# Ranking the experts of the second MoE on the chip: two short experts with weights fetched by computed address

## The chip, the cores and the metric

The kernel runs on one core of one Trainium2 chip. The metric is the device time of one execution in microseconds (us), as the median of several runs. A core has five engines that run side by side, each with a queue of its own that it works off in order: PE (TensorE, the matmuls; its weight loads are shown apart as PEld), DVE (VectorE), ACT (ScalarE), POOL (GpSimd) and SP (SyncE, which here only issues DMAs). Sixteen DMA engines move data for all queues.

## The reference: what is computed

Three stages follow each other, all in fp32. First comes an attention with 4 batches, 8 heads, 576 positions and head size 64, in which each query keeps its 32 largest scores. Its output, 2304 tokens of width 512, goes through a first "MoE" that has one expert for all tokens (512 to 2048 to 512). Then comes the second MoE, which the change is about:

```python
logits = x @ w_gate                       # 8 experts
expert_idx = np.argmax(logits, axis=1)    # one expert per token
...
for e in range(E):
    mask = expert_idx == e
    xe = x[mask]
    h = np.maximum(xe @ w1[e], 0.0)       # 512 -> 1024
    ye = h @ w2[e]                        # 1024 -> 512
    out[mask] = gate_w[mask, None] * ye
```

Evaluated on the inputs that it draws, the reference sends 328, 333, 249, 289, 285, 189, 284 and 347 tokens to experts 0 to 7.

## The kernel before, in words

**Precision.** A matmul of the MoE stages is made of three passes: each operand is split into a high part `h` and a low part `l` of type fp32r, and h·h, h·l and l·h are accumulated. ACT makes the high part and DVE the low part.

**First MoE (`l1` L829, `l2` L860).** Tokens are worked in blocks of 256, and the hidden width in 16 chunks of 128. One step is one chunk: 12 matmuls of 128x256 for layer 1 (4 chunks of the input width, 3 passes) and 6 matmuls of 128x512 for layer 2 (2 token tiles, 3 passes). Between the two, ACT takes layer 1 out of PSUM (`gf`, `epi_a` L835), DVE and POOL finish it. The weights of layer 2 are read back from DRAM in each step (`wo`, L815, 512 KB). After each block `gate` works out the expert of each token, its place in that expert's list and its gate weight; the token's row goes to DRAM (`yd`, L917, 516 floats a row) and its number to a table in DRAM (`td`, L938). Each expert has a list of 2304 places there.

**Second MoE (L1128 to L1229).** Each expert gets `SLOTS` = 3 slots of 128 tokens (`CAP` = 384). The first 128 x 3 entries of each list form a table of 24 columns, `tab`, one column for each slot. The entries of the earlier blocks are read from `td` (`load_table`, L951: two reads and their minimum on DVE, L955); those of the last block are added in PSUM: `placed` holds, for each of its two token tiles, a matrix that says the place in a slot and one that says the slot, and PE multiplies them (L1133, L1135). DVE turns the sum into integers (`tabg`, `tab`, L1136, L1137). Then for each expert, in the order 0 to 7:

- `xgather(e)` (L1141): POOL fetches three tiles of 128 token rows by an indirect DMA (L1148).
- `xprep(e, j)` (L1152): four PE transposes per slot (L1157), ACT and DVE make the high and low part (L1159, L1160).
- `m2l1(e, f)` (L1165) for 8 chunks f of the hidden width: 12 matmuls of 128x384 into `lp`, which has two buffers (L1175); then ACT (L1179) and DVE (L1180).
- `m2l2(e, f)` (L1187): for each of 3 slots 3 matmuls of 128x512 (L1192). It runs two chunks behind `m2l1`.
- `m2out(e)` (L1194): ACT scales the three outputs (L1198), POOL scatters them to `out` (L1199).

**Weights of the second MoE.** An expert's two matrices come in 8 pieces of 512 KB, even numbers from `w1` and odd ones from `w2`. `wpiece(e, i)` (L963) takes one of 3 `raw` buffers, issues the load on SP (L967, L970), and has ACT and DVE split it (L977, L978). Six pieces of expert 0 are asked for in the last steps of the first MoE (L1116 to L1122). Pieces 5 and 7 are asked for after it, since their split parts lie in memory that the first MoE holds until it ends. After that, step (e, f) of the second MoE asks for piece f of expert e + 1 (L1228).

**Order.** The program gives each instruction a priority and a scheduler lays each engine's queue out ahead of time, so an instruction can stand in its queue well ahead of where the source has it, if the scheduler expects its data by then. On the chip each queue is then worked off in that order.

**End.** `control` (L1234) adds up the number of tokens beyond the slots and two other flags; a register load (L1300) decides whether a slow path runs. There, `more(cs, e, n)` (L1249) computes what is left of expert e, 128 tokens at a time, with weights that it loads by itself.

Of the kernel before, what the change touches and what calls it, by code (L numbers as in the profile page):

```python
# [57 lines left out]
def attention_two_moe_kernel(  # L58
# [36 lines left out]
    SLOTS = 3  # L95
    CAP = SLOTS * P
    NCK = 8
    CK = S // NCK

# [54 lines left out]
    def constants():  # L154
# [30 lines left out]
        G.iota(first, pattern=[[NT, NE], [P, SLOTS]], base=0, channel_multiplier=0, allow_small_or_imprecise_dtypes=True)  # L185
        c["tokm"] = tokm = cpool.tile([P, NTT], F32, name="tokm")
        G.iota(tokm, pattern=[[P, NTT]], base=-NT, channel_multiplier=1, allow_small_or_imprecise_dtypes=True)
        c["wg"] = wg = cpool.tile([P, NCC, NE], F32, name="wg")
# [9 lines left out]
    def body(cs, exact):  # L198
# [672 lines left out]
        def gate(bk, tt, y):  # L871
# [52 lines left out]
            if last:  # L924

                ad2 = m1p.tile([P, 1], I32, tag="ad2", bufs=2, name=f"ad2{i}")
                place, in128 = [wp[0].tile([P, n], F32, tag=f"oh{n}", bufs=2, name=f"oh{n}_{i}") for n in (P, NSL)]
                V.tensor_scalar(ad2, ad, P - 1, None, op0=ALU.bitwise_and)
                V.tensor_copy(sc[:, 4:5], ad2)
                V.tensor_tensor(sc[:, 5:6], sc[:, 3:4], sc[:, 4:5], op=ALU.subtract)  # L930
                V.tensor_scalar(place, cs["row"], sc[:, 4:5], None, op0=ALU.is_equal)
                V.tensor_tensor(sc[:, 6:7], cs["tokm"][:, i:i + 1], sc[:, 3:4], op=ALU.subtract)
# [14 lines left out]

        NSL = NE * SLOTS
        placed, gdone, trows, tables = [], [0], [], []

        def load_table():  # L951
            trows.extend(wp[0].tile([NSL, P], F32, name=f"trow{i}") for i in range(2))
            for a_, t_ in zip(trows, td):
                SP.dma_start(a_, t_.rearrange("(e s p) o -> e s (p o)", e=NE, p=P)[:, 0:SLOTS, :])
            V.tensor_tensor(trows[0], trows[0], trows[1], op=ALU.min)  # L955

# [4 lines left out]
        wst = {}  # L961

        def wpiece(e, i):  # L963
            kind, pc = i % 2, i // 2
            raw = wp[0].tile([P, 4 * FW], F32, tag="raw", bufs=3, name=f"raw{e}_{i}")
            if kind == 0:
                SP.dma_start(raw.rearrange("p (c f) -> p c f", c=NCC),  # L967
                             w1[e, :, pc * FW:(pc + 1) * FW].rearrange("(c p) f -> p c f", p=P))
            else:
                SP.dma_start(raw.rearrange("p (j n) -> p j n", j=FPP),  # L970
                             w2[e, pc * FW:(pc + 1) * FW, :].rearrange("(j p) n -> p j n", p=P))
            late = kind and pc >= NPC // 2
# [137 lines left out]
        wp[0] = m2.enter_context(tc.tile_pool(name="wp" + X, bufs=1, side="right"))  # L1110
        pre = []
        while gpos[0] < NG + 3 or pend:
# [16 lines left out]
        tab = tabp[0].tile([P, NSL], I32, name="tab")  # L1129
        tabg = tabp[0].tile([P, NSL], I32, name="tabg")  # L1130
        tps = ps2.tile([P, NSL], F32, tag="tp", bufs=2, name="tps")
# [33 lines left out]
        def m2l1(e, f):  # L1165
# [4 lines left out]
            fs = slice((f % FPP) * P, (f % FPP + 1) * P)  # L1170
            lp = ps2.tile([P, CAP], F32, tag="lp", bufs=2, name=f"lp{e}_{f}")
# [5 lines left out]
            hh = tabp[0].tile([P, CAP], F32R, tag="hh", bufs=3, name=f"hh{e}_{f}")  # L1177
            hl = tabp[0].tile([P, CAP], F32R, tag="hl", bufs=3, name=f"hl{e}_{f}")
            A.activation(hh, lp, AF.Relu)  # L1179
# [5 lines left out]
        def m2l2(e, f):  # L1185
            hh, hl = hst.pop((e, f))
            h, l = wst[e, 1, f // FPP]  # L1187
            ns = slice((f % FPP) * DM, (f % FPP + 1) * DM)
            for j in range(SLOTS):
                js = slice(j * P, (j + 1) * P)  # L1190
# [3 lines left out]
        def m2out(e):  # L1194
            gw = xst[e][2]
            for j in range(SLOTS):
                o = tabp[0].tile([P, DM], F32, tag="osb", bufs=3, name=f"osb{e}_{j}")
# [15 lines left out]
        for s in range(len(seq) + 2):  # L1213
            if s < len(seq):
                e, f = seq[s]
                if e + 1 < NE:
                    if f == (e == 0):
                        xgather(e + 1)
                    if 4 <= f < 4 + SLOTS:
                        xprep(e + 1, f - 4)  # L1220
# [13 lines left out]
    def control(cs, X):  # L1234
        with ExitStack() as st:
            ps = st.enter_context(tc.tile_pool(name="ctlp" + X, bufs=1, space=PSUM)).tile([1, 2 + NE], F32, name="ctlp")
            ctl, f = cs["ctl"], cs["ctlf"]
            PE.matmul(ps[:, 0:2], cs["one"], cs["flag"], start=True, stop=True)
            PE.matmul(ps[:, 2:2 + NE], cs["ones"][:, 0:1], cs["ohsum"], start=True, stop=True)
            cnt, over = f[:, 2:2 + NE], f[:, 2 + NE:2 + 2 * NE]  # L1240
            V.scalar_tensor_tensor(cnt, cs["iota8"][0:1, :], -float(NT), ps[:, 2:2 + NE], op0=ALU.mult, op1=ALU.add)
            V.tensor_scalar(over, cnt, float(CAP), 0.0, op0=ALU.is_gt, op1=ALU.add, accum_out=f[:, 0:1])
            V.tensor_scalar(over[:, 0:2], ps[:, 0:2], 1.0, 0.0, op0=ALU.mult, op1=ALU.add, accum_out=f[:, 1:2])
# [5 lines left out]
    def more(cs, e, n):  # L1249
        ident = cs["ident"]  # L1250
        with ExitStack() as st:
# [3 lines left out]
            for nm, src, m in (("1", w1, DM // P), ("2", w2, F2 // P)):  # L1255
# [5 lines left out]
                ws.append((h, l))  # L1261
            with tc.For_i(CAP, n, P) as i:
                row = [wp.tile([P, 1], F32, name=f"row{t_}") for t_ in range(len(td))]
# [37 lines left out]
    with tc.If(todo > 0):  # L1301
# [4 lines left out]
        for e in range(NE):  # L1306
            n = nc.values_load(ctl[0:1, 2 + e:3 + e], min_val=0, max_val=NT)
            with tc.If(n > CAP):
                more(cs, e, n)
# [30 lines left out]
```

## Time and profile before

| | |
|---|---|
| median of 3 runs | 1249.9 us (1246.48 to 1253.28) |
| profiled execution, own time | 1248.94 us |
| its span, first to last instruction | 1247.0 us |
| granted TensorE clock, mean | 0.961 of 2.4 GHz |
| PE busy | 1148.2 us (92%) |
| DVE, ACT, POOL busy | 940.1, 816.1, 461.8 us |
| HBM traffic | 180 MB, 144 GB/s over the span |

The profile has a page with totals and can be asked for parts of the span. In the rows below, "start us, us" are the start from the beginning of the span and the duration; "[3.14 <-ACT wh L977]" says that the engine was idle for 3.14 us before the instruction and what it was released by. An x12 is a count. The attention ends at about 871 us, the first MoE at 932, and the second MoE's matmuls run from 956 to 1232.

### The profile page before, as it was taken

To read this page: it belongs to the slowest core of one execution; us is meant where nothing else is said; L and a number is where in the kernel's file an instruction comes from. 1 tells how busy PE (TensorE), PEld (TensorE's weight loads), DVE (VectorE), ACT (ScalarE), POOL (GpSimd) and SP (SyncE) were. 2 spreads that over 40 slices of the span, in tenths; PEclk is the share of its full clock that TensorE was granted. 3 is DMA by queue.
4 is the path that set the end of the run, shared out by engine and by line. 5 is a ranking of instruction groups with operands and counts; after the bars stand their busy time and mean duration, and the time that the engine had idled before them with its cause. 6 is when DMAs were issued, how large, how long until landed. Compare 5 with 4: busy or idle time off the path is not lost.

```text
span 1247.0 us, 23972 instructions
## 1 busy us (share of the span) xinstructions
PE 1148.2 (92%) x7453; PEld 1033.9 (83%) x7453; DVE 940.1 (75%) x3800; ACT 816.1 (65%) x2089; POOL 461.8 (37%) x670
## 2 busy tenths in 40 slices
PE   6676788999999999999999999999986999999995
PEld 4565677788999899999888899998875999999994
DVE  4999999999999999999897999995423444444420
ACT  4888778687888887787777887784422444444421
POOL 5886555743323534323433323223433112221100
PEclk9678799999999999999999999999996999999998
DMA  3654556555544655645435545444954455555300
GB/s 81 201 163 137 181 187 207 156 140 144 148 125 126 141 155 161 141 124 135 129 99 153 145 121 155 121 121 125 315 170 136 147 171 172 154 163 164 121 19 26
DMA packets 184665, 180.22 MB, mean 145 GB/s; under 512 B 123933, under 2 KB 148813, under 8 KB 184528
## 3 DMA queue, kind: packets, MB, share of 16 engines
q1 hardware_dynamic: 178960, 167.24, 46.4%
q0 software_dynamic: 4416, 11.08, 2.9%
q8 instruction: 61, 1.00, 0.3%
q14 instruction: 76, 0.62, 0.2%
q10 hardware_dynamic: 1152, 0.28, 0.1%
HBM read 160.52 MB, written 19.59 MB: 144 GB/s over the span
## 4 chain that ended last, share of the span: by engine, by line
PE 74%; DVE 14%; ACT 5%; DMA 3%; issue 2%; POOL 2%; SPq 0%; POOLq 0%; ACTq 0%; DVEq 0%
PE l1ps L829 13%; PE yps L860 13%; PE lp L1175 11%; PE ops L1192 11%; PE ptps L755 9%; PE sps L596 5%; PE ptps L721 4%; DVE cd L626 2%; DVE pbuf L705 2%; DVE z L662 2%; DVE z L697 1%; PE ptps L888 1%; DMA raw<-in_moe_w_dram 1%; PE misc L440 1%; PE tp L1157 1%
## 5 line engine op out<-in xcount | busy, mean ns | idle before, releaser
L860 PE MATMUL yps<-wo,gh 128*128 128x512 f32 x576 | 216.3, 416 | 0.1
L264 POOL TENSOR_SCALAR gh<-gf 128x256 fp32r<-128x256 f32 x144 | 74.9, 520 | 348.9 <-PE yps L860 224.4
L626 DVE MAX8 cd<-sbuf 128x8 f32<-128x72 f32 x1152 | 187.9, 218 | 3.0 <-ACT sbuf L266 2.7
L829 PE MATMUL l1ps<-xh,wih 128*128 128x256 f32 x576 | 167.7, 291 | 8.7 <-DVE gf L841 6.6
L829 PE MATMUL l1ps<-xh,wil 128*128 128x256 f32 x576 | 163.8, 284 | 0.0
L829 PE MATMUL l1ps<-xl,wih 128*128 128x256 f32 x576 | 163.6, 284 | 0.0
L978 DVE TENSOR_TENSOR wl<-raw,wh 128x1024 fp32r<-128x1024 f32 x64 | 79.4, 1245 | 93.6 <-ACT wh L977 91.7
L755 PE MATMUL ptps<-vn,pt 128*128 128x65 f32 (+1 forms) x1152 | 145.1, 280 | 0.0
L755 PEld LDWEIGHTS ptps<-vn,pt 128*128 128x128 f32 x1152 | 142.4, 200 | 0.0
L705 DVE SCALAR_TENSOR_TENSOR pbuf<-sbuf,tall,pbuf 128x576 f32<-128x576 f32 x144 | 137.2, 953 | 0.2
L849 POOL TENSOR_TENSOR gl<-gf,gh 128x256 fp32r<-128x256 f32 x144 | 124.8, 867 | 11.3
L829 PEld LDWEIGHTS l1ps<-xh,wih 128*128 128x128 f32 x576 | 110.0, 191 | 20.1 <-DVE gf L841 12.3
L977 ACT ACTIVATE wh<-raw 128x1024 fp32r<-128x1024 f32 x64 | 67.7, 1059 | 83.4 <-PE lp L1175 40.2
L860 PEld LDWEIGHTS yps<-wo,gh 128*128 128x128 f32 x576 | 107.2, 189 | 16.0 <-POOL qh L452 0.3
L860 PE MATMUL yps<-wo,gl 128*128 128x512 f32 x288 | 116.6, 405 | 0.6 <-POOL gl L849 0.6
L687 ACT ACTIVATE jk<-sbuf,uall 128x576 bf16<-128x576 f32 x144 | 111.6, 775 | 4.1 <-DVE j L701 0.9
L678 ACT ACTIVATE pbuf<-sbuf,nb 128x576 f32<-128x576 f32 x144 | 111.1, 775 | 4.1 <-PE ptps L723 0.9
L829 PEld LDWEIGHTS l1ps<-xl,wih 128*128 128x128 f32 x576 | 110.1, 191 | 4.1
L266 ACT ACTIVATE sbuf<-sps 128x576 f32<-128x576 f32 x144 | 93.0, 646 | 29.9 <-PE sps L596 17.9
L721 PE MATMUL ptps<-ident,pbuf 128*128 128x128 f32 x576 | 93.7, 285 | 18.1 <-DVE j L701 10.2
L829 PEld LDWEIGHTS l1ps<-xh,wil 128*128 128x128 f32 x576 | 110.3, 192 | 0.1
L596 PE MATMUL sps<-kx,qh 128*128 128x288 f32 (+2 forms) x336 | 95.8, 318 | 15.0 <-ACT sbuf L266 11.1
(206 smaller groups left out, 3043.0 us busy)
## 6 DMA issues: line engine op xcount, KB each, us to landing
wo<-wod SPq DMA_DIRECT2D x144, 512.0 KB
raw<-in_moe_w_dram SPq DMA_DIRECT2D x64, 512.0 KB
vn<-in_v_dram SPq DMA_DIRECT2D x96, 128.0 KB
rawi<-in_moe_w_in_dram SPq DMA_DIRECT2D x16, 512.0 KB
rawo<-in_moe_w_out_dram SPq DMA_DIRECT2D x16, 512.0 KB
wod<-wc SPq DMA_DIRECT2D x16, 512.0 KB
qn<-in_q_dram SPq DMA_DIRECT2D x126, 64.0 KB
yd<-y SPq DMA_DIRECT2D x18, 258.0 KB
```

Source lines behind the costliest of these rows:

```text
L596: PE.matmul(d_, a_, b_, start=(i == 0), stop=(i == len(mm) - 1))
L626: V.max(cd[:, c, :], s[:, c * CK:(c + 1) * CK])
L678: A.activation(d["p"], d["s"], AF.Exp, bias=d["nb"], scale=SCALE)
L687: A.activation(jk, d["s"][:, 0:S], AF.Sign, bias=ts[t]["u"], scale=-1.0, accum_out=d["sg"])
L705: V.scalar_tensor_tensor(d["p"], d["s"], tall[:, t:t + 1], d["p"], op0=ALU.is_ge, op1=ALU.mult)
L721: PE.transpose(ptps[:, c * P:(c + 1) * P], pb[:, c0 + c * P:c0 + (c + 1) * P], ident)
L755: PE.matmul(d_, a_, b_, start=(i == 0), stop=(i == len(mm) - 1))
L829: PE.matmul(dst, a[:, c, fs], b_[:, c, :], start=(n == 0), stop=(n == 3 * NCC - 1))
L849: G.tensor_tensor(gl, gf, r_(gh), op=ALU.subtract)
L860: PE.matmul(yps[tt], a[:, tsl], b_, start=(f == 0 and m == 0), stop=(f == NF1 - 1 and m == 2))
L1175: PE.matmul(lp, a[:, c, fs], b_[:, c, :], start=(n == 0), stop=(n == 3 * NCC - 1))
L1192: PE.matmul(ops_[j], a[:, js], b_[:, ns], start=(f == 0 and m == 0), stop=(f == NF2 - 1 and m == 2))
```

## The change

The experts are worked in order of rank: expert 0 always comes first, then the others from the largest token count to the smallest (ties by number). The last two ranks have 2 slots of 128, not 3. Which expert has which rank is computed on the chip, so from rank 1 on the weight loads take the expert's number from a register of SP.

In `constants`, `tokm` goes and five small tables come (two iotas on POOL, eight small DVE operations). `load_table` drops the minimum on DVE; PE adds both table reads instead. After the first MoE:

```diff
+        rk = ps2.tile([P, 256], F32, name="rk")
+        cnt = rk[0:NSL, 0:NE]
+        PE.matmul(cnt, ones[:, 0:NSL], ohsum, start=True, stop=True)
+        key = place_[:, 0:NE]
+        V.tensor_tensor(key, cnt, cs["bias"], op=ALU.add)
+        V.scalar_tensor_tensor(place_[:, NE:2 * NE], key, 1.0, own, op0=ALU.mult, op1=ALU.mult, accum_out=rank[:, 1:2])
+        V.tensor_scalar(place_[:, 2 * NE:3 * NE], key, rank[:, 1:2], 0.0, op0=ALU.is_gt, op1=ALU.add, accum_out=rank[:, 0:1])
+        V.tensor_scalar(rank[:, 2:3], rank[:, 0:1], float(SLOTS), part[:, 0:1], op0=ALU.mult, op1=ALU.add)
+        V.tensor_scalar(place_, cs["row"][0:NSL, 0:NSL], rank[:, 2:3], None, op0=ALU.is_equal)
+        tq = ps2.tile([NSL, P], F32, tag="tp", bufs=2, name="tq")
+        for i, a_ in enumerate(trows):
+            PE.matmul(tq, ident[0:NSL, 0:NSL], a_, start=(i == 0), stop=False)
+        for i, (a_, b_) in enumerate(placed):
+            PE.matmul(tq, b_, a_, start=False, stop=(i == len(placed) - 1))
+        V.scalar_tensor_tensor(trows[0], tq, part[:, 3:4], cs["row"][0:NSL, :], op0=ALU.subtract, op1=ALU.subtract)
         tps = ps2.tile([P, NSL], F32, tag="tp", bufs=2, name="tps")
-        PE.matmul(tps, trows[0], ident[0:NSL, 0:NSL], start=True, stop=False)
-        for i, (a_, b_) in enumerate(placed):
-            PE.matmul(tps, a_, b_, start=False, stop=(i == len(placed) - 1))
+        PE.matmul(tps, trows[0], place_, start=True, stop=True)
         V.tensor_scalar(tabg, tps, float(NT - 1), None, op0=ALU.min)
         V.tensor_copy(tab, tps)
+        PE.matmul(rk[0:1, 16:16 + NE], part[:, 1:2], place_.rearrange("p (e s) -> p e s", s=SLOTS)[:, :, 0], start=True, stop=True)
+        V.tensor_copy(cs["list"], rk[0:1, 16:16 + NE])
+        for r in range(1, NE):
+            turn[r] = nc.values_load(cs["list"][0:1, r:r + 1], engines=[mybir.EngineType.SP], min_val=0, max_val=NE - 1)
```

The load of a piece is parted from its split, and takes its address from `turn`:

```diff
+        def wload_(e, i, after=None):
+            kind, pc = i % 2, i // 2
+            at_ = slice(e, e + 1) if e == 0 else ds(turn[e], 1)
+            wraw[e, i] = raw = wp[0].tile([P, 4 * FW], F32, tag="raw", bufs=3, name=f"raw{e}_{i}")
+            if after is not None:
+                G.tensor_copy(raw[:, 0:1], after[:, 0:1])
+            if kind == 0:
+                SP.dma_start(raw.rearrange("p (c f) -> p c f", c=NCC),
+                             w1[at_, :, pc * FW:(pc + 1) * FW].rearrange("o (c p) f -> p (o c) f", p=P))
...
         def wpiece(e, i):
             kind, pc = i % 2, i // 2
...
+            if (e, i) not in wraw:
+                wload_(e, i)
+            raw = wraw.pop((e, i))
...
-            if gpos[0] > NG - 12 and len(pre) < NPC + NPC // 2:
-
-                pre.append(2 * len(pre) if len(pre) < NPC else 2 * (len(pre) - NPC) + 1)
-                wpiece(0, pre[-1])
+            if gpos[0] > NG - 13 and len(pre) < NPC + NPC // 2:
+
+                if len(wraw) == 3 or len(pre) + len(wraw) == NPC + NPC // 2:
+                    pre.append(order[len(pre)])
+                    wpiece(0, pre[-1])
+                if len(pre) + len(wraw) < NPC + NPC // 2:
+                    wload_(0, order[len(pre) + len(wraw)])
...
         xgather(0)
         for f_ in tables:
             f_()
+        for i in range(2 * NPC):
+            if i not in pre and (0, i) not in wraw:
+                wload_(0, i, xst[0][3][0])
         for i in range(2 * NPC):
             if i not in pre:
                 wpiece(0, i)
```

So pieces 5 and 7 of expert 0 are loaded only once the first gathered tile of expert 0 has arrived (`after`). In `xgather`, `xprep`, `m2l1`, `m2l2` and `m2out` the loops over slots and the widths follow the rank:

```diff
+    SHORT = 2
+    def slots(r):
+        return SLOTS - (r >= NE - SHORT)
...
+            w = slots(e) * P
+            lp = ps2.tile([P, CAP], F32, tag="lp", bufs=2, name=f"lp{e}_{f}")[:, 0:w]
...
-                    PE.matmul(lp, a[:, c, fs], b_[:, c, :], start=(n == 0), stop=(n == 3 * NCC - 1))
+                    PE.matmul(lp, a[:, c, fs], b_[:, c, 0:w], start=(n == 0), stop=(n == 3 * NCC - 1))
...
-            for j in range(SLOTS):
+            for j in range(slots(e)):
```

`control` counts a token as left over if it is beyond 384 in a long expert or beyond 256 in a short one; that takes one more small matmul on PE and three more DVE operations. `more` starts at place 256 for any expert that overflows.

## Rows read from the trace of the kernel before

**Rows 1.** The page: engines' totals, and the split of a weight piece on DVE.

```profile
PE 1148.2 (92%) x7453; PEld 1033.9 (83%) x7453; DVE 940.1 (75%) x3800; ACT 816.1 (65%) x2089; POOL 461.8 (37%) x670
...
L978 DVE TENSOR_TENSOR wl<-raw,wh 128x1024 fp32r<-128x1024 f32 x64 | 79.4, 1245 | 93.6 <-ACT wh L977 91.7
```

**Rows 2.** Windows: length, busy PE, PEld, DVE, ACT, POOL, PE clock, DMA share, GB/s.

```profile
940.00:950.00 10.00, 1.83 (x8) 1.53 (x7) 4.92 (x25) 2.00 (x2) 6.19 (x7) 0.50 0.52 90
...
1000.00:1100.00 100.00, 100.00 (x521) 90.57 (x520) 47.12 (x56) 44.87 (x65) 18.94 (x22) 1.00 0.51 157
```

**Rows 3.** Chain that ended last, 1000 to 1035 us: start, us, what.

```profile
1007.72 0.44 PE tp L1157 x4
...
1016.92 2.12 PE lp L1175 x12
...
1021.12 2.08 PE lp L1175 x12
...
1025.26 2.12 PE lp L1175 x12
```

**Rows 4.** Chain that ended last, 898 to 926 us.

```profile
922.24 1.39 PE yps L860 x6
923.62 1.42 PE l1ps L829 x12
```

**Rows 5.** Timeline of ACT, end of the first MoE.

```profile
904.34 0.48 ACT L835 ACTIVATE gf<-l1ps,three 128x256 f32<-128x256 f32 x1 [2.33 <-PE ptps L913]
...
910.28 1.06 ACT L977 ACTIVATE wh<-raw 128x1024 fp32r<-128x1024 f32 x1 [2.50 <-DMA raw<-in_moe_w_dram]
...
925.13 0.48 ACT L835 ACTIVATE gf<-l1ps,three 128x256 f32<-128x256 f32 x1 [2.33 <-PE l1ps L829]
...
943.77 2.00 ACT L977 ACTIVATE wh<-raw 128x1024 fp32r<-128x1024 f32 x2 [3.85 <-DMA td<-tok,ad]
...
966.02 1.06 ACT L977 ACTIVATE wh<-raw 128x1024 fp32r<-128x1024 f32 x1 [2.93 <-DMA raw<-in_moe_w_dram]
```

**Rows 6.** Timeline of DVE: table of slots, and an operation on 24x128.

```profile
922.46 0.28 DVE L955 TENSOR_TENSOR trow<-trow,trow 24x128 f32<-24x128 f32 x1 [1.97 <-DMA trow<-td]
...
941.66 0.69 DVE L933 TENSOR_SCALAR oh<-first,lsc 128x24 f32<-128x24 f32 x2
943.49 0.18 DVE L1136 TENSOR_SCALAR tabg<-tps 128x24 int32<-128x24 f32 x1 [1.14 <-DMA yd<-y]
```

**Rows 7.** Timeline of PE from the table to the second MoE.

```profile
940.75 0.59 PE L1133 MATMUL tps<-ident,trow 24*128 24x24 f32 x2 [0.45 <-DVE ad L923]
942.01 1.05 PE L1135 MATMUL tps<-oh,oh 128*128 128x24 f32 x4 [0.67 <-DVE oh L933]
950.86 1.09 PE L1157 MATMUL tp<-ident,xg 128*128 128x128 f32 x4 [7.80 <-POOL gw L1161]
952.67 2.25 PE L1157 MATMUL tp<-ident,xg 128*128 128x128 f32 x8 [0.72 <-DMA xg<-yd,tabg]
...
955.94 0.72 PE L1175 MATMUL lp<-xeh,wh 128*128 128x384 f32 x2
```

**Rows 8.** The register load at the end (L1300) on SP's queue: ns min/median/max.

```profile
L1300 SPq TENSOR_LOAD <-ctl x1: 554/554/554, 1234.2 to 1234.2; - x1
```

**Rows 9.** Timelines of POOL and SP: first gather, a weight load.

```profile
944.49 0.99 POOL L1148 DMA_INDIRECT xg<-yd,tabg  x1 [0.85 <-issue]
...
962.69 0.37 SPq L970 DMA_DIRECT2D raw<-in_moe_w_dram  x1
```

**Rows 10.** DMA queues in 950 to 956 us (packets, MB, share of 16 engines).

```profile
q0 software_dynamic: 305, 1.03, 49.8%
q1 hardware_dynamic: 750, 0.95, 43.9%
```

**Rows 11.** Timelines of DVE and POOL at the end.

```profile
1234.04 0.16 DVE L1245 CAST ctl<-ctlf 1x10 int32<-1x10 f32 x1
...
1234.40 0.97 POOL L1199 DMA_INDIRECT out_dram<-osb,tab  x1 [0.31 <-DVE ctl L1245]
```

More of the change, by code (lines that the diff above doesn't have):

```diff
@@ L96, in attention_two_moe_kernel @@
     CAP = SLOTS * P
+    SHORT = 2
+    NSL = NE * SLOTS
+    def slots(r):
+        return SLOTS - (r >= NE - SHORT)
     NCK = 8
@@ L185, in constants @@
         G.iota(first, pattern=[[NT, NE], [P, SLOTS]], base=0, channel_multiplier=0, allow_small_or_imprecise_dtypes=True)
-        c["tokm"] = tokm = cpool.tile([P, NTT], F32, name="tokm")
-        G.iota(tokm, pattern=[[P, NTT]], base=-NT, channel_multiplier=1, allow_small_or_imprecise_dtypes=True)
+        c["own"] = own = cpool.tile([NSL, NE], F32, name="own")
+        c["part"] = part = cpool.tile([NSL, 8], F32, name="part")
+        c["lead"] = lead = cpool.tile([NSL, NE], F32, name="lead")
+        c["bias"] = bias = cpool.tile([NSL, NE], F32, name="bias")
+        c["place"] = place = cpool.tile([NSL, NSL], F32, name="place")
+        G.iota(lead, pattern=[[-SLOTS, NE]], base=0, channel_multiplier=1, allow_small_or_imprecise_dtypes=True)
+        V.tensor_scalar(own, lead, float(SLOTS - 1), None, op0=ALU.is_le)
+        V.scalar_tensor_tensor(own, lead, 0.0, own, op0=ALU.is_ge, op1=ALU.mult)
+        V.scalar_tensor_tensor(place[:, 0:NE], lead, 1.0, own, op0=ALU.mult, op1=ALU.mult, accum_out=part[:, 0:1])
+        V.scalar_tensor_tensor(place[:, 0:NE], iota8[0:NSL, :], 1.0, own, op0=ALU.mult, op1=ALU.mult, accum_out=part[:, 1:2])
+        V.tensor_scalar(lead, lead, 0.0, None, op0=ALU.is_equal)
+        G.iota(part[:, 2:3], pattern=[[0, 1]], base=NT, channel_multiplier=NT // SLOTS, allow_small_or_imprecise_dtypes=True)
+        V.scalar_tensor_tensor(part[:, 3:4], part[:, 0:1], -float(NT - SLOTS * P) / SLOTS, part[:, 2:3], op0=ALU.mult, op1=ALU.add)
+        V.tensor_scalar(bias, iota8[0:NSL, :], -(NT + 1.0 / 16), None, op0=ALU.mult)
+        V.memset(bias[:, 0:1], 2.0 * NT)
+        c["list"] = cpool.tile([1, NE], I32, name="list")
         c["wg"] = wg = cpool.tile([P, NCC, NE], F32, name="wg")
@@ L961, in body @@
         wst = {}
+        wraw, turn = {}, {}
+        def wload_(e, i, after=None):
[7 more added lines that the diff above has]
+                             w1[at_, :, pc * FW:(pc + 1) * FW].rearrange("o (c p) f -> p (o c) f", p=P))
+            else:
+                SP.dma_start(raw.rearrange("p (j n) -> p j n", j=FPP),
+                             w2[at_, pc * FW:(pc + 1) * FW, :].rearrange("o (j p) n -> p (o j) n", p=P))
         def wpiece(e, i):
             kind, pc = i % 2, i // 2
[L965 to L971, printed above, removed]
+            if (e, i) not in wraw:
+                wload_(e, i)
+            raw = wraw.pop((e, i))
             late = kind and pc >= NPC // 2
@@ L1110, in body @@
         wp[0] = m2.enter_context(tc.tile_pool(name="wp" + X, bufs=1, side="right"))
-        pre = []
+        pre, order = [], [0, 2, 4, 6, 1, 3, 5, 7]
         while gpos[0] < NG + 3 or pend:
@@ L1188, in m2l2 @@
             ns = slice((f % FPP) * DM, (f % FPP + 1) * DM)
-            for j in range(SLOTS):
+            for j in range(slots(e)):
                 js = slice(j * P, (j + 1) * P)
@@ L1195, in m2out @@
             gw = xst[e][2]
-            for j in range(SLOTS):
+            for j in range(slots(e)):
                 o = tabp[0].tile([P, DM], F32, tag="osb", bufs=3, name=f"osb{e}_{j}")
@@ L1218, in body @@
                         xgather(e + 1)
-                    if 4 <= f < 4 + SLOTS:
+                    if 4 <= f < 4 + slots(e + 1):
                         xprep(e + 1, f - 4)
@@ L1235, in control @@
         with ExitStack() as st:
[L1236 removed]
+            ps = st.enter_context(tc.tile_pool(name="ctlp" + X, bufs=1, space=PSUM)).tile([1, 2 + 2 * NE], F32, name="ctlp")
             ctl, f = cs["ctl"], cs["ctlf"]
@@ L1239, in control @@
             PE.matmul(ps[:, 2:2 + NE], cs["ones"][:, 0:1], cs["ohsum"], start=True, stop=True)
+            V.tensor_scalar(cs["part"][:, 7:8], cs["part"][:, 4:5], NE - SHORT - 0.5, float(P), op0=ALU.is_gt, op1=ALU.mult)
+            PE.matmul(ps[:, 2 + NE:2 + 2 * NE], cs["part"][:, 7:8], cs["lead"], start=True, stop=True)
             cnt, over = f[:, 2:2 + NE], f[:, 2 + NE:2 + 2 * NE]
             V.scalar_tensor_tensor(cnt, cs["iota8"][0:1, :], -float(NT), ps[:, 2:2 + NE], op0=ALU.mult, op1=ALU.add)
-            V.tensor_scalar(over, cnt, float(CAP), 0.0, op0=ALU.is_gt, op1=ALU.add, accum_out=f[:, 0:1])
+            V.scalar_tensor_tensor(over, ps[:, 2 + NE:2 + 2 * NE], 1.0, cnt, op0=ALU.mult, op1=ALU.add)
+            V.tensor_scalar(over, over, float(CAP), 0.0, op0=ALU.is_gt, op1=ALU.add, accum_out=f[:, 0:1])
+            V.tensor_tensor(cnt, cnt, over, op=ALU.mult)
             V.tensor_scalar(over[:, 0:2], ps[:, 0:2], 1.0, 0.0, op0=ALU.mult, op1=ALU.add, accum_out=f[:, 1:2])
@@ L1261, in more @@
                 ws.append((h, l))
-            with tc.For_i(CAP, n, P) as i:
+            with tc.For_i((SLOTS - 1) * P, n, P) as i:
                 row = [wp.tile([P, 1], F32, name=f"row{t_}") for t_ in range(len(td))]
@@ L1307, in attention_two_moe_kernel @@
             n = nc.values_load(ctl[0:1, 2 + e:3 + e], min_val=0, max_val=NT)
-            with tc.If(n > CAP):
+            with tc.If(n > 0):
                 more(cs, e, n)
```

11 lines of the change are left out of this document (5 added, 6 removed).

## The prediction

> **What bounds the kernel now.** I read the page first, then the stretch of the second MoE by windows, then the chain of waits in it, and last the timelines of the two places where PE stands still.
>
> The page says that PE is busy 92% of the span, ahead of DVE with 75% [rows 1]. By windows, the second MoE is pure PE work: in 1000 to 1100 us PE is busy 100.00 of 100 us at full clock, DVE 47 and ACT 45 [rows 2]. The chain there alternates between layer 1 (12 matmuls, 2.08 to 2.12 us) and layer 2 (9 matmuls, the rest of a step); a step takes 4.17 us (4.20 from 1016.92 to 1021.12, then 4.14), and each gathered slot adds four transposes, 0.44 us [rows 3]. Whatever leaves PE's queue here leaves the time.
>
> PE stands still in two places. Near 910 us ACT waits for a weight piece to land (2.50 us) while the next `gf` stands behind it in ACT's queue, and PE waits for that `gf` [rows 5]. These are expert 1's first pieces, which the scheduler has drawn forward into the first MoE. Between 932 and 956 us the gate, the table and the first gathers run one after the other; in 940 to 950 us PE has 1.83 us of work and the clock is granted at 0.50, which is the 1.2 GHz level [rows 2].
>
> **The change part by part.**
>
> *Short experts.* 2 experts x 8 chunks = 16 steps. Each now has 12 matmuls of 256 columns and 6 of 512. That is exactly the mix of a step of the first MoE, and the trace has it: 1.42 + 1.39 = 2.81 us [rows 4]. So 4.17 - 2.81 = 1.36 us a step, 21.8 us in all, and 2 slots fewer to transpose, 0.9 us [rows 3]. PE is the bound here, so all of it counts: **-22.7**.
>
> The row says that 256 columns cost 0.118 us a matmul (1.42/12), 384 cost 0.174 (2.09/12 [rows 3]) and 512 cost 0.232 (1.39/6): proportional, no floor. The Trainium skill ("TensorE: Matmul & The Clock Gate", Back-to-back issue gap) gives another rule: the spacing of a stream is set by weight load and matmul together, about 81 ns at 128 columns and 131 ns at 512. By that slope, an estimate, 128 columns less would save only 17 ns a matmul, and layer 1 would give 3.2 us in place of 10.7. The trace disagrees at all three widths, so this gets the small chance below.
>
> *Pieces of expert 1.* Their address now comes from a register that is set only after the gate, so none can be drawn forward to 903 to 920 us. From the `gf` at 904.34 to the one at 925.13 are 6 steps, 20.79 us; undisturbed they would take 6 x 2.81 = 16.9 [rows 4, 5]. The stall of 3.9 us goes: **-3.9** (0 to -3.9). What is late next is nothing: with the loads gone only `wo` is fetched there. Loading expert 0's pieces earlier I cost at nothing: the scheduler already had them in the three `raw` buffers as soon as the attention's memory was free.
>
> *Table and ranking.* The table now takes one more round: DVE evicts 24x128 (0.28 by the operation of that shape), PE multiplies once more (0.59 for a matmul of 24 rows at the low clock), and PE hands to DVE (the matmuls of 942.01 end at 943.06, DVE starts at 943.49, so 0.43) [rows 6, 7]. That is 1.3. The two `placed` matmuls stream 128 columns, not 24; at the low clock four 128-column transposes take 1.09, so up to 0.5; I take 0.3. The ranking is one small matmul and five DVE operations of some 0.18, about 1.0; DVE idles 1.14 before `tabg` [rows 6], which covers most of it; if not, 1.0. I take 0.4. Sum **+2.0** (1.0 to 2.9). Everything behind `tabg` waits for this, the gathers first of all.
>
> *Register loads.* Seven on SP, each 0.55 [rows 8]: 3.9 us, and with some register arithmetic 4 to 5, after one more matmul and copy. Queued behind them on SP are pieces 5 and 7 of expert 0 and all later pieces; the gathers go through POOL and do not wait. SP is free again near 952 us.
>
> *Gathers.* From the issue of the first (944.49) to its transposes (950.86) pass 6.4 us [rows 7, 9], while in 950 to 956 us weight loads move 0.95 MB beside the gathers' 1.03 [rows 10]. Now pieces 5 and 7 wait for the first gather (by a copy on POOL, behind which stand only the gathers of the next expert) and the others for the registers. At the 0.33 MB/us that both moved, 0.95 MB is worth 2.9 us at the most. PE then is held by its own transposes and their evictions: of the stretch from 950.86 to 955.94 only 0.72 is spent waiting for a gather outright [rows 7]. I take half a microsecond more for the first gather itself: **-1.2** (0 to -2.9).
>
> *Late pieces.* Pieces 5 and 7 were split at 943.77 in the idle time [rows 5]. Now they are loaded near 952, land some 3.3 us later (issue 962.69, ACT 966.02 [rows 5, 9]), and the split, 1.06 on ACT [rows 5] and 1.2 on DVE [rows 1], lies beside PE-bound work. They are needed in step 6, about 25 us after the start; the two `lp` buffers give ACT about 2 us of slack. If they stand ahead of the first evictions in ACT's queue, PE waits for them: 0 to +8; I take **+0.7**, nearer to nothing, since a load of unknown landing is usually covered in rows such as the 2.93 at 966.02, where PE stayed busy.
>
> *Pieces for the last expert* have to come at one per 2.8 us, not 4.17. One turn of a buffer is 3.3 + 1.06 + 1.2 = 5.6 us, three buffers, so 1.9 us a piece. Enough, but ACT's waits of up to 2.93 us eat most of the slack: **+0.5** (0 to +11).
>
> *Start and end.* Eight small DVE operations at the start lie in DVE's wait for the first loads: 0 (to +1.3, eight of 0.16). At the end one scatter fewer takes 1.0 off POOL, but beside a slot of PE's that is 0.7 shorter and counted above, so 0.3 to 0.6 is left; `control` gets chained DVE operations of 0.16 and a matmul more, +0.5 [rows 11]. 0 (-0.6 to +0.6).
>
> **Sum:** -22.7 - 3.9 + 2.0 - 1.2 + 0.7 + 0.5 = -24.6. The profiled execution took 1248.9 (span 1247.0 and 1.9 around it), 1.0 below the median of 1249.9; from the one the sum gives 1224.3, from the other 1225.3. I say **1225**.
>
> **The rivals.**
>
> *The hand-over becomes the loss.* SP's register loads and the late pieces push the first steps back, pieces 5 and 7 stand before the first evictions on ACT: +10 over my terms, 1235. For it: ACT's queue is laid out ahead, and at 910 us it did wait in this way. Against it: the scheduler knows that these pieces come after the gather. 12%.
>
> *The seventh expert starves.* With 2.8 us steps the pieces of the eighth come late, ACT waits, and the step stays at 4.17: half of the 21.8 is lost, 1236. For it: ACT waits for `raw` today. Against it: 1.9 us a piece by the buffers, and the first MoE fetches 512 KB of `wo` in each 2.81 us step. 8%.
>
> *Weight loads set a floor under short matmuls.* 7.5 us less gain, 1232. The measured 1.42 for 12 speaks against it; 2%.
>
> *The slow path runs: slower.* The point is the 257th token in an expert of rank 7 or 8. Then `more` comes after the end: 4.2 MB of weights at 0.33 MB/us 12.7 us, splitting them 8 x 1.2 = 10, gather 6.4, transposes and evictions 2.4, 96 matmuls at 0.118 or less and 24 at 0.232 some 17, scatter 3: about 51 us, so 1276. For it: the mean is 288 tokens, and 249 is 7 away from 256. Against it: on its own inputs the reference's smallest counts are 249 and 189, and the trace of before has no instruction of `more`, so no expert was above 384. 3%.
>
> *More than I count* (the whole 2.9 of the gathers, a shorter end): below 1219, 3%.
>
> **How the numbers follow.** The forecast case has 72%, with 1219 to 1231 as its own range. To leave out no more than 2 in 10 the range goes from 1218 to 1236, so that it takes in the two cases at 1235 and 1236. A difference of 0.5%, 6 us, is about what can be told from no change here. Faster by more than that (below 1243.7): all cases but the slow path and the two losses together, 0.94; within it 0.03; slower 0.03.
>
> **What would show it.** Right: matmuls of 128x256 at L1175's successor, 64 per pass, 1.4 us per 12; short experts of some 23.5 us against 34.7; no weight piece on ACT from 900 us to the end of the first MoE, and `gf` every 2.81 there; `tabg` some 2 us after its old distance from the last DVE operation of the gate; seven register loads on SP, under 6 us. Wrong: PE idle inside the second MoE, longest where ACT waits for `raw`; a first `lp` over 16.6 us behind the last DVE operation of the gate (now 942.35 to 955.94, 13.6 [rows 6, 7]); any instruction of the slow path.

## The result, and the profile after

| | before | after |
|---|---|---|
| median (range) | 1250.7 us (1246.48 to 1253.28, 6 runs) | 1222.7 us (1216.34 to 1229.23, 6 runs) |
| span of the profiled execution | 1247.0 us | 1221.1 us |
| PE busy | 1148.2 us | 1127.4 us |

The changed kernel takes 0.9778 of the time before (95% interval 0.9756 to 0.9800). Predicted were 1225.0 us, with a range of 1218 to 1236: the measured 1222.7 us lies inside.

The two spans differ by 25.9 us. I cut both at events that both have: two `gf` of the first MoE on ACT, the first `lp` on PE, and the end of PE's last `ops`.

| stretch | before | after | difference |
|---|---|---|---|
| start to a `gf` of the first MoE | 872.79 | 874.29 | +1.50 |
| that `gf` to the last one | 55.16 | 51.54 | -3.62 |
| last `gf` to the first `lp` | 27.99 | 27.30 | -0.69 |
| first `lp` to the end of PE's work | 276.21 | 253.20 | -23.01 |
| rest | 14.85 | 14.77 | -0.08 |

The first row holds the attention, which the change leaves alone; in experiment 7 below, whose first two stages are the same, the last `gf` comes 2.7 us earlier than here, and I explain nothing with that row.

**The gates.** ACT's timeline at the end of the first MoE, where one `gf` came 20.79 us after another six steps earlier [rows 5]:

```profile
902.99 0.47 ACT L854 ACTIVATE gf<-l1ps,three 128x256 f32<-128x256 f32 x1 [1.95 <-PE l1ps L848]
905.80 0.47 ACT L854 ACTIVATE gf<-l1ps,three 128x256 f32<-128x256 f32 x1 [2.34 <-PE ptps L932]
...
923.02 0.47 ACT L854 ACTIVATE gf<-l1ps,three 128x256 f32<-128x256 f32 x1 [2.35 <-PE l1ps L848]
925.83 0.47 ACT L854 ACTIVATE gf<-l1ps,three 128x256 f32<-128x256 f32 x1 [2.34 <-PE l1ps L848]
```

Now they follow each other by 2.81 to 2.99 us, six steps take 17.22 us (905.80 to 923.02), and PE waits for none of them.

**The hand-over**, from the last `gf` of the first MoE to the first `lp` of the second. The counterparts of [rows 6, 7] and of the first gather in [rows 9], from the timelines of DVE, POOL and PE, and the register loads on SP's queue (ns min/median/max):

```profile
939.71 0.69 DVE L952 TENSOR_SCALAR oh<-first,lsc 128x24 f32<-128x24 f32 x2
...
942.42 0.18 DVE L1181 TENSOR_SCALAR tabg<-tps 128x24 int32<-128x24 f32 x1 [0.74 <-PE tps L1180]
...
943.42 0.99 POOL L1197 DMA_INDIRECT xg<-yd,tabg  x1 [1.74 <-DVE list L1184]
...
948.42 1.94 PE L1206 MATMUL tp<-ident,xg 128*128 128x128 f32 x8 [5.98 <-issue]
951.33 1.97 PE L1206 MATMUL tp<-ident,xg 128*128 128x128 f32 x8 [0.96 <-DVE xel L1209]
953.13 1.01 PE L1225 MATMUL lp<-xeh,wh 128*128 128x384 f32 x2
...
L1186 SPq TENSOR_LOAD <-list x7: 262/264/481, 942.8 to 946.5; - x7
```

From the last operation of the gate (its end, 940.40) to `tabg` pass 2.02 us, before 1.14. From the first gather to the transposes pass 5.00, before 6.37; from there to the first `lp` 4.71, before 5.08. The chain that ended last shows what comes next:

```profile
940.73 5.77 DMA td<-tok,ad
946.49 1.93 issue
948.42 1.10 PE tp L1206 x4
...
953.30 5.99 PE lp L1225 x24
```

The first 24 `lp` take 5.99 us, where at full clock they take 4.17. The granted clock in 942 to 954 us is 0.50, the 1.2 GHz level. PE's timeline shows where it rises; below are two neighbouring rows from the changed kernel, then from experiment 2, then from experiment 1:

```profile
956.58 0.45 PE L1225 MATMUL lp<-xeh,wh 128*128 128x384 f32 x1
956.87 0.34 PE L1225 MATMUL lp<-xel,wh 128*128 128x384 f32 x1
```

```profile
953.55 0.45 PE L1225 MATMUL lp<-xeh,wl 128*128 128x384 f32 x1
953.84 0.34 PE L1225 MATMUL lp<-xeh,wh 128*128 128x384 f32 x1
```

```profile
956.89 0.40 PE L1179 MATMUL lp<-xel,wh 128*128 128x384 f32 x1
957.13 0.34 PE L1179 MATMUL lp<-xeh,wl 128*128 128x384 f32 x1
```

Up to the first row of each pair the `lp` start 0.32 us apart or more, behind the second 0.17 to 0.18. So not all 24 are slow: of the changed kernel's the first eleven are. In the trace of the kernel before only the first gap is longer; its first 24 take 4.4 us, so the two traces differ by 1.6 us here. That this comes from the change is not shown. Experiment 2, with the changed kernel's hand-over, has seven slow `lp` from its first at 951.38 on; experiment 1, with the hand-over of the kernel before, has eleven from 953.12 on.

**The second MoE.** Groups of PE by line and shape from 1000 to 1207 us, the window from the first 256-column matmul to the end of PE's work (columns as in [rows 2]), and ACT's waits for weight pieces (total, times, longest):

```profile
L1242 PE MATMUL ops<-wh,hh 128*128 128x512 f32 x148 | 57.9, 391 | 0.0
L1225 PE MATMUL lp<-xeh,wh 128*128 128x384 f32 x144 | 49.5, 344 | 0.0
L1225 PE MATMUL lp<-xeh,wh 128*128 128x256 f32 x64 | 18.1, 283 | 0.0
```

```profile
1156.36:1206.33 49.97, 49.97 (x315) 44.67 (x313) 16.61 (x27) 17.64 (x31) 5.21 (x7) 1.00 0.25 82
```

```profile
ACT wh L1005 <- DMA raw<-in_moe_w_dram: 25.1, 18, 2.7
```

PE is busy in 49.97 of 49.97 us: ACT waits 25.1 us for pieces in all, and none of it reaches PE. One short step starts at 1163.35, the next at 1166.15: 2.80 us.

### The profile page after: what moved, and what is told of

Same layout as the page of the kernel before. It is cut to its first block, busy times and chain, and to the rows that moved or that the text cites. A ratio compares the mean times of both kernels' runs of the same rounds, so it can differ in the third digit from the quotient of the medians.

```text
span 1221.1 us, 24014 instructions
## 1 busy us (share of the span) xinstructions
PE 1127.4 (92%) x7406; PEld 1015.4 (83%) x7406; DVE 936.6 (77%) x3819; ACT 810.8 (66%) x2085; POOL 456.5 (37%) x667
## 4 chain that ended last, share of the span: by engine, by line
PE 67%; DVE 17%; issue 7%; ACT 4%; POOL 2%; DMA 1%; SPq 0%; POOLq 0%; ACTq 0%
PE l1ps L848 14%; PE yps L879 13%; PE ptps L774 9%; PE lp L1225 7%; PE ops L1242 7%; PE sps L615 5%; PE ptps L740 4%; DVE cd L645 3%; DVE pbuf L724 3%; DVE z L681 2%; DVE z L716 2%; PE ptps L907 1%; DVE cw L656 1%; DVE m L651 1%; PE misc L459 1%
## 5 line engine op out<-in xcount | busy, mean ns | idle before, releaser
L868 POOL TENSOR_TENSOR gl<-gf,gh 128x256 fp32r<-128x256 f32 x144 | 124.6, 865 | 11.4
L854 ACT ACTIVATE gf<-l1ps,three 128x256 f32<-128x256 f32 x144 | 67.9, 471 | 64.2 <-PE l1ps L848 53.3
```

The lines of the kernel that those rows point to most:

```text
L868: G.tensor_tensor(gl, gf, r_(gh), op=ALU.subtract)
```

## The experiments

Of the twelve kernels the first two take the change apart, the next four look at the gates and the slow path, the rest at the hand-over and at one difference that I had not foreseen.

**1. Short experts alone.** The kernel before, experts 2 and 5 fixed at two slots, nothing ranked.

```diff
+    def slots(e):
+        return SLOTS - (e in (2, 5))
```

> The kernel before, in which experts 2 and 5 (the two with 249 and 189 tokens) get 2 slots by a fixed rule: no ranking, no computed address, order and loads as before. Theory (the time comes from the columns of PE, stage by stage): 16 steps of 1.36 us and 2 slots of transposes fewer, 22.7 us less, so a ratio of 0.982, about 1228 us; the stall of PE near 910 us (3.1 us in two waits for gf) stays. Rival (the short slots give the whole gain, the loads nothing): 0.978, like the change. Rival (short experts cannot be fed: their pieces come late): above 0.987, with PE idle in experts 2 and 5 or behind them.

Measured: 1226.5 us, ratio 0.982 (0.9806 to 0.9834), which is 22.5 us. The stall in the gates is still there (PE waits for `gf` 2.3 us).

**2. Everything but the short experts.** The changed kernel with `SHORT = 0`.

> The changed kernel with no short expert (all ranks have 3 slots): ranking, table by two rounds, register loads, computed addresses and the gated loads of pieces 5 and 7 remain. Theory: the stall of 3.6 us at the end of the first MoE is gone, the hand-over is some 0.7 us shorter, so 4 to 6 us less than before, ratio 0.995 to 0.997; the first 24 matmuls of layer 1 run at the low clock as in the changed kernel. Rival (the ranking costs about what it saves): ratio 0.999 to 1.002. Rival (much more of the gain is here than in the short slots): below 0.993.

Measured: 1243.2 us, ratio 0.9957 (0.9942 to 0.9971). The two ratios multiplied give 0.9778, that of the whole change: the parts add up. One point of the expectation fell: seven `lp` ran at the low clock, not 24.

**3. Expert 1's early pieces taken away from the kernel before.**

```diff
+            if e == 1 and i < 3:
+                G.tensor_copy(raw[:, 0:1], xst[0][3][0][:, 0:1])
```

> The kernel before, in which the loads of expert 1's first three pieces wait for the first gathered tile of expert 0 (a copy on POOL), nothing else. Theory: no weight piece of expert 1 is left in the queue of ACT before the end of the first MoE, gf comes every 2.81 us there and PE's wait for gf (3.1 us) is gone, so 3 to 5 us less, ratio 0.996 to 0.9975. Rival (the stall comes from something else and goes elsewhere): ratio 0.999 to 1.001, with the same sum of idle time. If the late pieces then stall the first steps of the second MoE, PE waits there and the gain is given back.

Measured: ratio 0.9991 (0.9978 to 1.0004). The theory fell. The wait for the piece is gone, but another has come. DVE's timeline, and PE's waits from 900 to 930 us (total, times, longest):

```profile
915.89 0.42 DVE L841 SCALAR_TENSOR_TENSOR gf<-gf,l1ps 128x256 f32<-128x256 f32 x1 [2.54 <-ACT gf L835]
921.38 0.28 DVE L955 TENSOR_TENSOR trow<-trow,trow 24x128 f32<-24x128 f32 x1 [5.07 <-DMA trow<-td]
921.59 0.40 DVE L841 SCALAR_TENSOR_TENSOR gf<-gf,l1ps 128x256 f32<-128x256 f32 x1
```

```profile
PE l1ps L829 <- DVE gf L841: 2.6, 1, 2.6
```

The minimum of the two table reads (L955) stands in DVE's queue ahead of the next `gf` and waits 5.07 us for the read of `td`. In the kernel before it stood in the shadow of the piece; the row was there, 922.46 [rows 6], and I had read only its duration.

**4. and 5. The other wait alone, and both.** In experiment 4 PE adds the two reads, as the changed kernel does, and one small DVE subtraction behind it takes the place of the minimum; in 5 the copy of experiment 3 stands beside it.

```diff
-            V.tensor_tensor(trows[0], trows[0], trows[1], op=ALU.min)
...
+        for i, a_ in enumerate(trows):
+            PE.matmul(tps, a_, ident[0:NSL, 0:NSL], start=(i == 0), stop=False)
```

> The kernel before, with its two partial tables summed by TensorE at the transposition in place of VectorE's minimum (line 955), as the changed kernel does; the pieces of expert 1 still wait for the first transposes. One more small VectorE operation stands ahead of the gathers (about 0.2 us). Theory A (both waits, the piece and the minimum, cover the same 3 to 4 us of the gates, so that removing one alone brings nothing): the wait of TensorE for gf near 910 to 925 us stays at 2.5 to 4 us and the ratio is 0.999 to 1.001. Rival (the minimum alone makes the stall): the wait goes, gf follows gf by 2.8 us throughout, ratio 0.996 to 0.998.

> The kernel before with both: the minimum replaced by a sum on TensorE, and the first three pieces of expert 1 loaded only when the first gathered tile is there. Theory A: the stall in the gates is gone, gf follows gf by 2.8 us from 905 to 926 us, a gain of 3 to 3.6 us, ratio 0.9965 to 0.998 (0.2 us of it given to the added operation, some to colder first matmuls of expert 0). Rival (a third thing stands behind the second wait): a gap of over 4 us between two gf's stays, ratio 0.999 to 1.001.

Measured: 4 alone 1.0011 (1.0002 to 1.002); both 0.9978 (0.9965 to 0.9992). PE's waits from 900 to 930 us, the longest row of the one, with a row of its ACT timeline, then of the other:

```profile
PE l1ps L831 <- DVE gf L843: 2.4, 2, 1.8
...
914.20 1.06 ACT L978 ACTIVATE wh<-raw 128x1024 fp32r<-128x1024 f32 x1 [2.77 <-DMA raw<-in_moe_w_dram]
```

```profile
PE misc L882 <- ACT y L869: 0.7, 1, 0.7
```

In experiment 4 ACT still waits for the piece with the next `gf` (915.17) behind it. So the two waits cover the same stretch, and either is enough to keep it; the traces show this in both directions, while the ratios of experiments 3 and 5 overlap. Of the 3.6 us in the gates 2.8 are left in the time (1.0 to 4.4 by the interval). From the first `lp` to the end the kernel with both needs 2.5 us more than the kernel before. Of it 0.7 us is a wait of `lp` for `hl`, and 0.16 us per expert is a longer period (34.87 for 34.71 us), perhaps of the kind of experiment 10, which was not tested here; the rest stays open.

**6. The slow path.** The changed kernel with `SHORT = 3`: the expert of rank 5 has 284 tokens for 256 slots, and `more` runs for it.

> The changed kernel with three short experts: rank 5 has 284 or 285 tokens, so 28 or 29 are beyond its 256 places and the slow path runs for this expert. Theory: 11.4 us less in PE's queue than the change, and about 51 us more for one pass of the slow path, so about 1262 us, slower than before. Rival (the slow path is cheap, its loads and splits overlap): under 1240. Rival (starting it costs more, since its code and the branch come on top): over 1280.

Measured: 1299.0 us, ratio 1.0398 (1.038 to 1.0417). A third short expert alone would give 1222.7 - 11.4 (half of what two save), so the slow path costs 88 us; I had priced 51. Windows from `control` to the end (columns as in [rows 2]):

```profile
1196.00:1223.00 27.00, 0.34 (x5) 0.22 (x5) 1.41 (x11) 0.00 (x0) 0.20 (x1) 0.51 0.06 17
1223.00:1260.00 37.00, 9.29 (x36) 8.09 (x36) 10.46 (x8) 8.38 (x5) 0.98 (x1) 0.50 0.34 121
1260.00:1298.00 38.00, 24.80 (x91) 21.56 (x89) 1.75 (x6) 2.35 (x7) 1.00 (x1) 0.50 0.01 3
```

For 27 us, up to the first weight load at 1223.08, next to nothing runs but a second `control` at 1201.6 to 1203.5; the trace does not name what fills the rest. And the clock stays at 0.50 to the end: the eight chunks take 4.04 us each, 32 us for my 17. These two are 42 us more than I had, where 37 are missing, so the rest of the path took some 5 us less than priced.

**7. Pieces 5 and 7 not held back.** The changed kernel with `wload_(0, i)` in place of `wload_(0, i, xst[0][3][0])`.

> The changed kernel with the late pieces (5 and 7) of expert 0 loaded as soon as their buffers are free, not behind the first gathered tile. Theory (the rows of the kernel before: gathers 6.4 us from issue to transposes with two pieces of 512 KB in flight): the gathers land 1 to 1.5 us later than in the changed kernel's 5.0 us, and TensorE's first transposes with them, ratio against before 0.978 to 0.980. Rival (the transfers do not hold the gathers, the scatters of the table ahead of them on GpSimd's queue do): the gathers stay at 5.0 us, ratio 0.977 to 0.979 and the trace without a difference there.

Measured: 1222.4 us, ratio 0.9809 (0.9789 to 0.9829), an interval that overlaps that of the changed kernel. Its trace shows more than the time. POOL's issue of the first gather, and PE's transposes:

```profile
939.78 2.47 POOL L1197 DMA_INDIRECT xg<-yd,tabg  x1 [1.73 <-ACT wh L1005]
...
944.93 1.09 PE L1206 MATMUL tp<-ident,xg 128*128 128x128 f32 x4 [6.11 <-issue]
947.04 1.09 PE L1206 MATMUL tp<-ident,xg 128*128 128x128 f32 x4 [1.02 <-DMA xg<-yd,tabg]
951.11 1.09 PE L1206 MATMUL tp<-ident,xg 128*128 128x128 f32 x4 [2.98 <-DMA xg<-yd,tabg]
952.72 1.09 PE L1206 MATMUL tp<-ident,xg 128*128 128x128 f32 x4 [0.52 <-DMA xg<-yd,tabg]
```

The first gather (issued 939.78) lands about as late as in the changed kernel, but the later ones do not. Three pieces are issued on SP from 943.60 on, and the third and fourth gather, issued behind the first of them, take 7.15 and 7.51 us to land, against 4.23 and 4.49 in the changed kernel. The first `lp` comes 13.7 us after the first gather, against 9.7, and behind it 0.6 us comes back. The fourth gather lands 12.8 us after the first is issued, not 8.3: 3.0 us of that are its longer flight beside the pieces. The other 1.5 are no matter of the pieces as far as the trace shows, since POOL took 2.47 us to issue the first gather, not 0.99, before any piece left. So holding the pieces back is worth 2 to 3.4 us in the traces; the times alone don't show it.

**8. and 9. The last scatters of the table behind the gathers.** In the changed kernel two scatters to `td`, which only the slow path reads, stand on POOL ahead of the gathers; the chain above names them with 5.77 us. Now they wait for the third gathered tile. The first try put a copy of the token numbers into a new tile, the second writes them in place.

```diff
+                    V.scalar_tensor_tensor(tok[:, i:i + 1], x[:, 0:1], 0.0, tok[:, i:i + 1], op0=ALU.mult, op1=ALU.add)
...
-            f_()
+            f_(xst[0][3][2])
```

> The changed kernel with the last two scatters of the table (needed by the slow path alone) held until the third gathered tile is there, so that they are behind the gathers on GpSimd's queue. Theory (the rival of the run before this): the gathers land 1 to 2 us sooner, transposes at most 4 us behind the gather's issue, ratio against before 0.976 to 0.9775. Rival (the gathers' time is that of their own rows): 5.0 us as before, no difference.

> The late scatters again, without a new tile, so that every tile lies where it does in the changed kernel. Theory (the first try gained 1.5 us at the gathers and lost 1.7 us by the layout): gathers to transposes 3.5 us against 5.0, period of a full expert 34.39 us, ratio against before 0.975 to 0.977. Rival (the late pieces, not the layout, took the gain back): period 34.67 us again or the gathers at 5 us, ratio 0.978.

Measured: 0.9782 (0.9769 to 0.9795) and 0.9776 (0.9758 to 0.9795): no difference from the changed kernel, so both theories fell in their ratio. The transposes do come sooner, 3.5 and 3.4 us after the first gather and not 5.0, but the first `lp` hardly does (8.8 and 9.3, not 9.7). PE's timeline of the second try, with its first gather issued at 944.28:

```profile
947.66 1.09 PE L1208 MATMUL tp<-ident,xg 128*128 128x128 f32 x4 [4.35 <-issue]
949.29 1.09 PE L1208 MATMUL tp<-ident,xg 128*128 128x128 f32 x4 [0.54 <-DMA xg<-yd,tabg]
950.92 1.09 PE L1208 MATMUL tp<-ident,xg 128*128 128x128 f32 x4 [0.55 <-DMA xg<-yd,tabg]
952.85 1.09 PE L1208 MATMUL tp<-ident,xg 128*128 128x128 f32 x4 [0.83 <-DMA xg<-yd,tabg]
953.58 0.99 PE L1227 MATMUL lp<-xeh,wh 128*128 128x384 f32 x2
```

Each set of four waits for its own gather, and the fourth, which is expert 1's first tile, stands in PE's queue ahead of the first `lp`. That gather is issued 3.85 us behind the first and takes 4.58. So in these two kernels the last of four gathers sets the start, not the first; in the changed kernel PE's last wait before the first `lp` is the 0.96 us for `xel` at 951.33. Another order on PE was not tried.

**10. One unused tile of 64 bytes.** A full expert takes 34.71 us in the kernel before (`osb` at 993.87, 1028.58, 1063.29), but 34.39 in the changed kernel and in experiment 2, though the instructions are the same; in the first late-scatter kernel it took 34.67.

```diff
+        tabp[0].tile([P, 16], F32, name="pad")
```

> The changed kernel with one unused tile of 64 bytes per partition set aside behind the gathered tiles, so that hh, hl and the late pieces' wh and wl lie 64 bytes higher, as in the run with the late scatters; not an instruction is added or moved. Theory (the 34.39 us period of a full expert, against 34.71 in the kernel before, hangs on where these tiles lie: 34.71 with hh at byte 77120, 34.87 at 77312, 34.67 at 77344, 34.39 at 77280): the period becomes 34.67 us, the mean of the 512-column matmuls 394 to 395 ns instead of 391, six full experts lose 1.7 us, ratio against before 0.979 to 0.980. Rival (the order of the scatters and gathers made it): the period stays at 34.39 us.

Measured: ratio 0.9785 (0.9765 to 0.9805), too close to tell by time. ACT's timeline has two `osb` of the changed kernel and then two of this one, and below them is this one's group of 512-column matmuls:

```profile
1026.81 0.68 ACT L1248 ACTIVATE osb<-ops,gw 128x512 f32<-128x512 f32 x1
1061.20 0.68 ACT L1248 ACTIVATE osb<-ops,gw 128x512 f32<-128x512 f32 x1
```

```profile
1025.48 0.68 ACT L1248 ACTIVATE osb<-ops,gw 128x512 f32<-128x512 f32 x1
1060.14 1.26 ACT L1248 ACTIVATE osb<-ops,gw 128x512 f32<-128x512 f32 x2
```

```profile
L1242 PE MATMUL ops<-wh,hh 128*128 128x512 f32 x146 | 57.7, 395 | 0.0
```

34.39 and 34.66 us, 391 and 395 ns: the trace follows the theory. An unused tile that moves `hh`, `hl` and the late pieces by 64 bytes costs 0.27 us per full expert. The other traces of variants of the changed kernel bear this out: experiments 2, 6, 7, 9, 11 and 12, without a new tile there, have 34.39 us; 8 and 10, with one, have 34.66 to 34.67. Which of these tiles it is was not tried. That the 34.71 us of the kernel before are layout too is likely but not shown: there this group takes 391 ns as well, and the other two (`wl,hh` and `wh,hl`) take 394 to 395, for 392 and 390 in the changed kernel.

**11. and 12. Work for PE while it waits.** Matmuls whose result nobody reads, between the table and the transposes: 20 of them, then 12.

```diff
+        wm = placed[0][0]
+        V.tensor_scalar(wm, cs["row"], tps[:, 0:1], None, op0=ALU.is_equal)
+        for _ in range(20):
+            PE.matmul(rk[:, 128:256], ident, wm, start=True, stop=True)
```

> The changed kernel with 20 matmuls of 128 columns without use (their result is read by nobody) between the table and the first transposes, where TensorE otherwise waits 6 us for the gathers. Theory (the first 24 lp matmuls ran at 1.2 GHz because TensorE had hardly worked in the 15 us before): transposes and first lp's run at the full clock or nearly, 1.4 to 2.4 us less from the first gather to the end of TensorE's work, ratio against before 0.976 to 0.978. Rival (the clock stays low in spite of it, or the added matmuls hold up the transposes): first lp's still 0.32 us apart, no gain or up to 2 us more.

> The changed kernel with 12 matmuls without use in place of the 20 of the run before, with which ScalarE's and VectorE's queues stand in the changed kernel's own order again (with 20, the split of a late piece had come to stand ahead of the third tile's evacuation, and TensorE waited 2.1 us there and was cold again). Theory (the cold clock is all that is at stake): transposes from 948.4 us on, as in the changed kernel, first lp's 0.17 us apart, not 0.32, 1.5 to 2.5 us less from the first gather to the end of TensorE's work, ratio against before 0.976 to 0.977. Rival (a low clock at the first lp's in spite of the work ahead of them, or a later gather takes the place): no difference from the changed kernel, ratio 0.978.

Measured with 20: 1226.3 us, 0.9809 (0.9783 to 0.9835). With 12: 1220.2 us, 0.9769 (0.9753 to 0.9785). PE's timeline with 20, then its timeline and windows with 12:

```profile
946.11 6.83 PE L1191 MATMUL rk<-oh,ident 128*128 128x128 f32 x40 [0.56 <-DVE oh L1189]
952.77 1.04 PE L1211 MATMUL tp<-ident,xg 128*128 128x128 f32 x8
955.18 1.25 PE L1211 MATMUL tp<-ident,xg 128*128 128x128 f32 x8 [1.38 <-DVE xel L1214]
958.58 1.01 PE L1230 MATMUL lp<-xeh,wh 128*128 128x384 f32 x2 [2.14 <-ACT xeh L1213]
```

```profile
949.37 1.07 PE L1211 MATMUL tp<-ident,xg 128*128 128x128 f32 x8 [1.15 <-issue]
951.81 1.26 PE L1211 MATMUL tp<-ident,xg 128*128 128x128 f32 x8 [1.38 <-DVE xel L1214]
```

```profile
948.00:954.00 6.00, 3.27 (x21) 2.12 (x20) 2.15 (x4) 2.28 (x4) 4.49 (x10) 0.98 0.93 292
954.00:960.00 6.00, 6.00 (x26) 5.91 (x27) 3.35 (x4) 2.50 (x3) 2.19 (x3) 0.74 0.90 311
```

In both the clock rises for the transposes (with 12 it is 0.98 in 948 to 954 us) and is low again at the first `lp` (with 20) or from the third on (with 12): PE has waited 1.2 us ahead of the transposes and 1.4 us among them with 12, 1.4 us among them and 2.1 us behind them with 20. With 20, ACT's queue also has a late piece's split ahead of a tile's evacuation, which is the 2.14. And the 20 hold the transposes up, as the rival had it: they end where the transposes begin, 6.25 us after the first gather, not 5.00. With 12 the first `lp` comes 8.9 us after the first gather, not 9.7, and nothing is won behind it. The theory, a full clock at the first `lp`, fell both times. The count of slow first `lp` moves without such help too: it is six in experiment 10 and 14 in experiment 9, whose kernels have no added work for PE. 0.9769 can't be told from 0.9778, so no kernel here is shown to beat the changed one.

## Why the prediction was right, and which steps of it failed

The mechanism that carries most of the time, fewer columns through a PE that is the bound, was right and is shown. The sum was -24.6; the two traces without their first stretch differ by 27.4 us, the medians by 28.0. The 2.8 us between are small terms that I had set too unfavourably: 1.1 for the table, 0.5 for the gathers, 1.2 for the late pieces and the last expert.

- *Short experts, -22.7*: right, and shown by doing them alone (22.5). The 64 matmuls of a pass, the 2.80 us step and 100% busy PE are as forecast. The 12 matmuls of 256 columns come at the price of the first MoE's, 0.118 us apart. The rival drawn from the Trainium skill ("TensorE: Matmul & The Clock Gate", Back-to-back issue gap) would have made the gain 7.5 us smaller, since by the slope of the page's two figures, an estimate, they would be about 0.098 us apart; the trace disagrees with it at this width too.
- *Pieces of expert 1, -3.9*: the size is right, -3.62 (undisturbed, six steps there take 17.2 us, not 16.9), but **the reason given was half of it**, and the size was met by luck. The failed step is "What is late next is nothing". Next was the minimum of the table reads, and removing the pieces alone brings nothing. The change took both away, and I had costed the dropped minimum at nothing without asking what stood behind it on DVE.
- *Table and ranking, +2.0*: measured +0.88, below the lower bound of 1.0. The ranking's operations lie for the most part among the gate's and beside PE's work, and the added round of PE and DVE took less than the sum of its parts.
- *Register loads*: 0.26 us each and 0.48 for the longest, not 0.55, and 4.2 us in all with the arithmetic between them. SP was free at 947.0, not 952; the late pieces left at 948.40, when the first gather had landed.
- *Gathers, -1.2*: the hand-over from gather to first `lp` measured -1.74 (-1.37 and -0.37). Experiment 7, without the holding back of pieces 5 and 7, keeps the first part (5.15 us to the transposes) and loses the second: 8.5 us from there to the first `lp`, not 4.7. So the loads beside the gathers are shown as a cost for the later gathers. Experiments 8 and 9 show one more cost that I had not named, the scatters of the table ahead of the gathers: 1.5 us of the first one.
- *Late pieces, +0.7* and *last expert, +0.5*: neither shows. PE waits for no split and for no piece.
- *Not foreseen, and of opposite sign*: the first eleven `lp` at the low clock, +1.6, and six full experts at 34.39 for 34.71 us, -1.9. That the stretch of the second MoE came out at -23.0, so near to -22.7, is luck in part, since these two cancel; the first is not shown to belong to the change at all.
- *The slow path*: rightly given 3%, wrongly priced. I priced its work at full clock and no entry; 27 us ahead of the first load and the low clock account for the 88 us in place of 51, and a little more.

## What to carry to other kernels

Before a stall is booked as gained, look in every engine's queue for the next instruction that waits in the same stretch: two waits that cover each other are worth nothing one at a time. In experiments 8 and 9 the gathers were as late as the last one that stood ahead of the first `lp` in PE's queue, so speeding up the first moved little. Before a stretch at the low clock is booked to a change, look at it in the traces of other kernels with the same code there: here its length went from one `lp` to 14. And a change that adds or drops a small tile moves the others: differences of 1% in a matmul's mean can be the layout, and an unused tile is enough to find out.

## What the hardware showed that I had not expected

- The 512-column matmuls of high by high part took 391 or 395 ns on average with the same instructions in the same order, depending on 64 bytes in the place of the tiles (a full expert 34.39 or 34.66 us).
- The clock, once at 2.4 GHz for the transposes, was back at 1.2 GHz from the third `lp` on after waits of 1.2 and 1.4 us, with 4.4 us of added matmuls ahead of them (experiment 12).
- How many of the first `lp` ran at 1.2 GHz did not follow the code of the hand-over: eleven in the changed kernel, seven in experiment 2 and six in experiment 10, which have the same one; one in the kernel before and eleven in experiment 1, which have the other.
- A number loaded into a register of SP costs 0.26 us when several follow each other, half of the single load at the end [rows 8].
- Between `control` and the slow path's first weight load lay 27 us in which no engine had over 1.41 us of work.
